# Pooling K and V in two chunked parts, six column copies per unit, and one pair's copies made a unit later or earlier, in a pooled attention with a top-1 mixture of experts

## The chip, the core and the metric

The kernel runs on one core of one Trainium2 chip. The time is the device time of one launch in microseconds (us). The core has a matrix engine (PE), a vector engine (DVE), a scalar engine (ACT), GpSimd (POOL) and a queue engine (SP) that here only issues DMAs. Each engine works through its own list of instructions strictly in order, and waits on semaphores for the others. A wait at the head of such a list holds everything behind it.

## The reference

```python
def _attn_ref(q, k, v):                       # (8, 8, 576, 64) each
    B, H, S, D = q.shape
    Sp = S // 8
    scale = 1.0 / np.sqrt(D)
    k_p = k.reshape(B, H, Sp, 8, D).mean(axis=3)
    v_p = v.reshape(B, H, Sp, 8, D).mean(axis=3)
    scores = scale * np.matmul(q, k_p.transpose(0, 1, 3, 2))
    scores = scores - np.max(scores, axis=-1, keepdims=True)
    attn = np.exp(scores)
    attn = attn / (np.sum(attn, axis=-1, keepdims=True) + 1e-09)
    return np.matmul(attn, v_p)
def _moe_ref(x, w_gate, w1, w2):              # x (4608, 512), 8 experts, F = 1024
    logits = x @ w_gate
    expert_idx = np.argmax(logits, axis=1)
    ...                                       # softmax, gate_w of the chosen expert
        h = np.maximum(x_sorted[lo:hi] @ w1[e], 0.0)
        y_sorted[lo:hi] = h @ w2[e]
    ...
    return (gate_w[:, None] * y)
```

Attention runs over keys and values that are means of eight rows. Its output, one row per token, goes through the one expert that a gate picks.

## The kernel before

**Two stages.** The attention stage takes roughly the first 200 us. It is a loop over 36 units: four pairs of batches, nine units a pair. Units 9g to 9g+3 hold the first batch of pair g, the next four the second batch, and the ninth the left-over rows of both. The loop's steps are numbered the same way below ("unit 18" is the first unit of batch 4). Six units (later four and two) make a routing group: their tokens' experts are found and their rows scattered to a buffer in HBM by expert. After that come blocks of 256 rows of one expert each, the expert stage, in a loop on the chip.

**The order of work** is written out by hand. A table of hooks says at which unit and at which place in it a step is issued: `"q"` at the unit's start (pooling on POOL), `"pe"`, `"act"`, `"dve"` in it, `"sp"` after the product with V. Small steps of routing and of V's columns stand in a list of fillers, and `fill()` issues the next one at set places. At every first unit of a routing group (6, 12, 18, 24, 30), `u_nrm` calls `drain`, which issues all that is left of an earlier group's fillers at once, and what stands ahead of them too.

**K and V of a batch.** `load_kv` (L250, L253) brings 1.1 MB of K or V into one of three buffers. `pool` (L328) adds eight rows to one on POOL, in three adds that halve the data: 1280, 640 and 320 numbers per partition. It is called in two parts, in two successive units. Batches 2 to 7 are pooled this way, K and V apart, so twelve times. Then PE turns the result (`k_pe`, `v_pe`), and `u_pe`, `u_dve` fold the gate's weights into V: `v_dve` (L402), `cross` (L418), `gather`, `high`, `low` (L429). `low` runs on POOL, and is the last step that makes `vc`. This text calls it `low` of a batch.

**V's columns.** The product with V needs `vc` spread out by head into one of three buffers `VB`. That is twelve small DMAs a batch, in the list `moves`, which `low` fills. A thirteenth one copies half of K's block (`bd<-bd`). After a unit's loads, the loop issues up to four of these (eight from unit 30 on) on SP. All loads of K, V, q (`load_q`, L257) and weights (`wload`, L102) are issued by SP too, in program order. Before unit 30 nothing but this order decides what a load stands behind.

**Also on POOL:** scatters of rows (`scatter`, L701 and L702), parts of the splits of weights into two half-precision parts (`wsplit`, L124 and L125), and `apart` (L605, L606): a pair of memsets put between two scatters when no pooling and no split came between them.

**Early block.** Under a condition that holds here, SP reads the first block of rows (L917) in unit 29, between the copies of batch 7.

Of the kernel before, what the change touches and what calls it, by code (L numbers as in the profile page):

```python
# [13 lines left out]
OP = mybir.AluOpType  # L14
# [18 lines left out]
def kernel(  # L33
# [10 lines left out]
    nc = tc.nc  # L44
    B, H, S, D = q.shape
# [182 lines left out]
    def row(x):  # L228

        return x[..., 0:ID].rearrange("p j (h x) -> p j h x", x=HW)[..., 0:D]  # L230

    def col(h):
        return h.rearrange("p j (h x) -> p j h x", x=D)
# [38 lines left out]
    for c in range(5):  # L272
        src = w_gate.rearrange("(h d) e -> d h e", d=D)[:, HS[c]:HS[c] + 3, :]
# [26 lines left out]
    moves = []  # L300

    def fill(n=1):
        while n and fillers and not fillers[0][1]:
            fillers.pop(0)[2]()
            n -= 1

    def fill_pe():
        if fillers and fillers[0][1]:
            fillers.pop(0)[2]()
# [9 lines left out]
    t1 = st[:, 0:1280].rearrange("p (c x) -> p c x", c=5)  # L319
    t2 = st[:, 1280:1920].rearrange("p (c x) -> p c x", c=5)  # L320
# [6 lines left out]

    def pool(src, dst, what=(0, 1)):  # L328
        last_pool[:] = []
        if 0 in what:  # L330
            nc.gpsimd.tensor_tensor(t1, src[:, :, 0:4 * D], src[:, :, 4 * D:], op=OP.add)
        if 1 in what:
            nc.gpsimd.tensor_tensor(t2, t1[:, :, 0:2 * D], t1[:, :, 2 * D:], op=OP.add)
            nc.gpsimd.tensor_tensor(dst, t2[:, :, 0:D], t2[:, :, D:], op=OP.add)

    def pool_now(src, dst, part):
# [128 lines left out]
    def g_qt(G, j):  # L465
        b, r = units[groups[G][0]]
        pq = psA.tile([128, 512], F32, name="pq", bufs=2)
        for x in range(4):
            if r is None:
                src = ql[(b // 2) % 2][:, 2 * x:2 * x + 2, :].rearrange("p h d -> p (h d)")  # L470
            else:
                src = qt[b % 2][:, 4 * j + x, r:r + 2, :].rearrange("p r d -> p (r d)")
            nc.tensor.transpose(pq[:, x * 128:(x + 1) * 128], src, ident)
        if j == 0:
            QT[G] = work.tile([128, 8, 128], F32, name="qT", bufs=2)
        nc.scalar.activation(QT[G][:, 4 * j:4 * j + 4, :].rearrange("p h t -> p (h t)"), pq, AF.Copy)
# [4 lines left out]
    def g_s(G, j):  # L481
        b, r = units[groups[G][0]]
        ps = psA.tile([128, 512], F32, name="ps", bufs=2)
        t = QT[G]
        if r is None:
            for x in range(2 * j, 2 * j + 2):
                for s in range(2):
                    bd = BD[(b + s) % 3].rearrange("p s h x -> p (s h) x")
                    rhs = bd[:, 2 * x:2 * x + H + 2:H + 1, :]
                    nc.tensor.matmul(ps[64 * s:64 * s + 64, (x % 2) * 2 * KP:(x % 2 + 1) * 2 * KP],  # L490
                                     t[:, x, 64 * s:64 * s + 64], rhs, start=True, stop=True)
            slots = [(4 * j + x, 0) for x in range(4)]
        else:
            hs = range(2 * j, 2 * j + 2)
            for x, h in enumerate(hs):
                nc.tensor.matmul(ps[:, x * 2 * KP:(x + 1) * 2 * KP], t[:, h, :],  # L496
                                 BD[b % 3][:, :, h, :], start=True, stop=True)
            slots = [(h, s) for h in hs for s in range(2)]
        PS_[G, j] = (ps, slots)
        if j == stages(G) - 1:  # L500
            QT.pop(G)

    def g_min(G, j):
        ps, slots = PS_[G, j]
        nmx = work.tile([128, 4], F32, name="nmx", bufs=4)
        nc.vector.tensor_reduce(nmx, ps[:, 0:4 * KP].rearrange("p (h x) -> p h x", x=KP), axis=AX.X, op=OP.min)  # L506
        PS_[G, j] = (ps, nmx, slots)

    def g_exp(G, j):
        ps, nmx, slots = PS_.pop((G, j))  # L510
        for x, (h, s) in enumerate(slots):
            p = pbuf[groups[G][s] % 4]
            nc.scalar.activation(p[:, h * KP:(h + 1) * KP], ps[:, x * KP:(x + 1) * KP], AF.Exp,  # L513
                                 bias=nmx[:, x:x + 1], scale=-1.0)

    def u_pt(i):
        p = pbuf[i % 4]
        pp = psA.tile([128, 1024], F32, name="pp")
        for c in range(5):
            nc.tensor.transpose(pp[:, c * 128:(c + 1) * 128], p[:, c * 128:(c + 1) * 128], ident)  # L520
        ph = work.tile([128, 640], F16, name="ph")
        nc.scalar.activation(ph, pp[:, 0:640], AF.Copy, scale=SP)
        PP_[i] = (pp, ph)

    def u_lo(i):
        pp, ph = PP_[i]
        pl = work.tile([128, 640], F16, name="pl", bufs=1)
        nc.vector.scalar_tensor_tensor(pl, pp[:, 0:640], SP, ph, op0=OP.mult, op1=OP.subtract)
        PP_[i] = (ph, pl)
# [67 lines left out]
    def flush(n=99, upto=99):  # L597
        while n and pend and pend[0][0] <= upto:
            _, f, u = pend.pop(0)
            f(u)  # L600
            n -= 1
# [143 lines left out]
    def pooled(n, b):  # L745
        KVS[n, b] = work.tile([128, 5, D], F32, name=n, bufs=2)
        return kv[(2 * b + (n == "vp")) % 3], KVS[n, b]
# [11 lines left out]
    src, vp = pooled("vp", 0)  # L759
# [55 lines left out]
    def put(i, pos, f, *a):  # L815
        assert 0 <= i < NU
        hooks.setdefault((i, pos), []).append((f, a))

    def prep(b, k, v, u):
        put(k[0], "pe" + k[1], k_pe, b)  # L820
        put(k[0], "act" + k[1], k_act, b)
        put(v[0], "pe" + v[1], v_pe, b)
        put(v[0], "act" + v[1], v_act, b)
        put(u[0], "pe" + u[1], u_pe, b)
        put(u[0], "dve", u_dve, b)
# [9 lines left out]
    for g in range(NPAIR):  # L835
        u0 = 9 * g
        e, o = 2 * g, 2 * g + 1
        if g:
            for b, at, last in ((e, u0 - 11, u0 - 8), (o, u0 - 7, u0 - 3)):
                first = 1 if (g == 1 and b == e) else 0  # L840
                for f, x in ((pool_k, 0), (pool_v, 2)):
                    if first:
                        put(1 + x // 2, "q", f, b, 0)
                        put(1 + x // 2, "q", f, b, 1)
                    else:
                        put(at + x, "q", f, b, 0)
                        put(at + x + 1, "q", f, b, 1)
                    n = 2 * b + x // 2 + 3
                    if n < 2 * B:
                        put(at + x + 4, "sp", load_kv, *order[n])  # L850
                if first:
                    prep(b, (3, "2"), (4, ""), (5, ""))
                else:
                    prep(b, (last, ""), (last + 1, ""), (last + 2 + (b == o), ""))
        if g + 1 < NPAIR:
            put(u0 + 1, "sp", load_q, e + 2)
            put(u0 + 6, "sp", load_q, o + 2)
            put(u0 + 5, "sp", load_ql, g + 1)
# [79 lines left out]
    def run(i, pos):  # L938
        for f, a in hooks.pop((i, pos), []):
            f(*a)  # L940

    def routes(i):
        gidx, u = GOF[i]
        if u == bounds[gidx][1] - 1:
            return route(gidx)
# [33 lines left out]
    for i in range(NU):  # L979
        A, Z = halves.get(2 * i), halves.get(2 * i + 1)  # L980
        Y = halves.get(2 * i - 1)
        run(i, "q")
        flush(1)
        if i:
            u_pt(i)
        if A:
            g_s(*A)
        if Y:
            g_exp(*Y)
        if i in turns:  # L990
            g_qt(*turns[i])
        if (i, "pe") not in hooks:
            fill_pe()
        run(i, "pe")
        if i:
            u_lo(i)
        if A:
            g_min(*A)
            fill()
            g_exp(*A)  # L1000
        fill()
        run(i, "act")
        run(i, "dve")
        if i:
            u_pv(i)
        run(i, "pe2")
        if i == 29:
            KVS["late"] = 1
        if len(pend) > 2:
            flush(1)  # L1010
        fill_pe()
        run(i, "sp")
        for _ in range(min(4 if i < 30 else 8, len(moves))):
            nc.sync.dma_start(*moves.pop(0))
        if Z:
            g_s(*Z)
        u_nrm(i, (lambda: g_min(*Z)) if Z else None)
        run(i, "act2")
        run(i, "dve2")
        last = routes(i)  # L1020
        fill(2 if i >= NU - 3 else 1)
# [177 lines left out]
    for j in range(2):  # L1199
        x, h, l = row(xg[:, j:j + 1]), col(xh[:, j:j + 1, 0]), col(xh[:, j:j + 1, 1])  # L1200
# [114 lines left out]
```

## Time and profile before

| | us |
|---|---|
| median of 3 runs | 645.25 |
| lowest, highest | 642.09, 645.43 |
| the profiled execution's own time | 646.38 |
| its span, first to last instruction | 644.4 |

The span is what the trace covers. The 2 us between it and the execution's own time lie around the program. The profiled execution is 1.1 us above the median of the runs. Times "at" some us below count from the start of the span.

### The profile page before, as it was taken

To read this page: it belongs to the slowest core of one execution; us is meant where nothing else is said; L and a number is where in the kernel's file an instruction comes from. 1 tells how busy PE (TensorE), PEld (TensorE's weight loads), DVE (VectorE), ACT (ScalarE), POOL (GpSimd) and SP (SyncE) were. 2 spreads that over 40 slices of the span, in tenths; PEclk is the share of its full clock that TensorE was granted. 3 is DMA by queue.
4 is the path that set the end of the run, shared out by engine and by line. 5 is a ranking of instruction groups with operands and counts; after the bars stand their busy time and mean duration, and the time that the engine had idled before them with its cause. 6 is when DMAs were issued, how large, how long until landed. Compare 5 with 4: busy or idle time off the path is not lost. (4 is left out here: it accounts for less than half of the span.)

```text
span 644.4 us, 15871 instructions
## 1 busy us (share of the span) xinstructions
PE 579.3 (90%) x4694; PEld 422.3 (66%) x4695; DVE 316.9 (49%) x619; ACT 286.8 (45%) x635; POOL 276.4 (43%) x532
## 2 busy tenths in 40 slices
PE   6888898787977698998899999999999989999994
PEld 5777788676865275675566667766667666677662
DVE  7577678886675417221773755122722262221212
ACT  2576688677651226222672753122722352221222
POOL 6799689998684323112314123222121232012212
PEclk9798999899899699999899999999999989999998
DMA  8997789858476565963689497533231333213200
GB/s 244 290 287 222 231 231 311 266 176 248 168 214 232 192 120 152 384 164 85 168 247 327 108 321 251 153 102 77 42 81 53 96 72 102 49 57 79 65 16 30
DMA packets 104203, 108.15 MB, mean 168 GB/s; under 512 B 62310, under 2 KB 72550, under 8 KB 104168
## 3 DMA queue, kind: packets, MB, share of 16 engines
q1 hardware_dynamic: 97528, 86.72, 47.9%
q0 software_dynamic: 6640, 20.99, 8.8%
q8 instruction: 19, 0.31, 0.2%
q14 instruction: 16, 0.13, 0.1%
HBM read 72.99 MB, written 23.37 MB: 150 GB/s over the span
## 5 line engine op out<-in xcount | busy, mean ns | idle before, releaser
L1039 PEld LDWEIGHTS <-bd 128*128 128x128 f16 x936 | 91.6, 99 | 110.1 <-issue 3.6
L1224 POOL TENSOR_TENSOR spacer<-ql,iG 1x1 f32<-1x1 f32 x44 | 23.8, 540 | 218.9 <-ACT ql L1220 218.0
L1033 DVE SCALAR_TENSOR_TENSOR bd<-ps,bd 128x512 f16<-128x512 f32 x44 | 30.2, 690 | 151.3 <-ACT bd L1029 149.5
L1033 DVE SCALAR_TENSOR_TENSOR bd<-pp,bd 128x512 f16<-128x512 f32 x44 | 30.3, 691 | 100.7 <-ACT bd L1029 100.7
L513 ACT ACTIVATE both<-ps,nmx 128x72 f32<-128x72 f32 x288 | 69.0, 330 | 23.9 <-DVE nmx L506 23.3
L1029 ACT ACTIVATE bd<-pp 128x512 f16<-128x512 f32 x44 | 26.2, 597 | 116.8 <-PE pp L969 74.3
L1039 PE MATMUL po<-w,bd 128*128 128x512 f16 x264 | 59.1, 379 | 0.8 <-ACT bd L1029 0.8
L1029 ACT ACTIVATE bd<-ps 128x512 f16<-128x512 f32 x44 | 26.1, 597 | 74.8 <-PE L967 46.1
L1039 PE MATMUL po<-kv,bd 128*128 128x512 f16 x264 | 58.9, 379 | 0.3 <-ACT bd L1029 0.3
L1225 POOL DMA_INDIRECT out_dram<-ql,iG x44 | 43.8, 995 | 21.5 <-issue 20.2
L496 PE MATMUL ps<-bd,qT 128*128 128x144 f32 x256 | 47.0, 310 | 3.5 <-DMA bd<-bd 1.9
L967 PE MATMUL ps<-kv,qt 128*128 128x256 f16 (+1 forms) x176 | 45.7, 267 | 4.9 <-issue 3.2
L1039 PE MATMUL pq<-kv,bd 128*128 128x512 f16 x216 | 48.1, 379 | 0.0
L969 PE MATMUL ps<-kv,qt 128*128 128x256 f16 (+1 forms) x176 | 45.6, 267 | 1.9 <-DVE qt L118 1.9
L967 PE MATMUL ps<-kv,w 128*128 128x256 f16 (+1 forms) x176 | 43.8, 262 | 3.1 <-DVE kv L118 2.8
L969 PE MATMUL ps<-kv,w 128*128 128x256 f16 (+1 forms) x176 | 43.8, 262 | 2.5 <-DVE w L118 2.5
L968 PE MATMUL ps<-kv,qt 128*128 128x256 f16 (+1 forms) x176 | 45.7, 267 | 0.0
L1039 PE MATMUL pq<-w,bd 128*128 128x512 f16 x192 | 45.3, 395 | 0.3 <-remote 0.3
L554 PE MATMUL po<-vb,ph 128*128 128x146 f16 (+2 forms) x384 | 33.4, 234 | 12.6 <-DMA vb<-vc 7.0
L969 PE MATMUL pp<-kv,qt 128*128 128x256 f16 (+1 forms) x176 | 44.7, 263 | 0.0
L968 PE MATMUL pp<-kv,qt 128*128 128x256 f16 (+1 forms) x176 | 44.7, 263 | 0.0
L967 PE MATMUL pp<-kv,qt 128*128 128x256 f16 (+1 forms) x176 | 44.7, 263 | 0.0
(236 smaller groups left out, 1335.8 us busy)
## 6 DMA issues: line engine op xcount, KB each, us to landing
both<-in_moe_w_dram SPq DMA_DIRECT2D x6, 2048.0 KB, 11.7
st<-in_moe_w_dram SPq DMA_DIRECT2D x6, 2048.0 KB
vb<-x_by_expert SPq DMA_DIRECT2D x17, 578.0 KB
st<-in_moe_w_dram SPq DMA_DIRECT2D x8, 1024.0 KB
kv<-in_k_dram SPq DMA_DIRECT2D x7, 1024.0 KB
kv<-in_v_dram SPq DMA_DIRECT2D x7, 1024.0 KB
qt<-in_q_dram SPq DMA_DIRECT2D x6, 1024.0 KB
qt<-in_q_dram SPq DMA_DIRECT2D x4, 512.0 KB
```

Source lines behind the costliest of these rows:

```text
L496: nc.tensor.matmul(ps[:, x * 2 * KP:(x + 1) * 2 * KP], t[:, h, :], BD[b % 3][:, :, h, :], start=True, stop=True)
L513: nc.scalar.activation(p[:, h * KP:(h + 1) * KP], ps[:, x * KP:(x + 1) * KP], AF.Exp, bias=nmx[:, x:x + 1], scale=-1.0)
L554: nc.tensor.matmul(po[:, half, cols], a[:, c * 128:(c + 1) * 128], VB[b % 3][:, y, c, sl, 0:CW], start=st, stop=False, skip_group_check=True)
L967: nc.tensor.matmul(dst, wh, xT[:, d, 0:n], start=(d == 0), stop=False)
L968: nc.tensor.matmul(dst, wh, xT[:, DC + d, 0:n], start=False, stop=False)
L969: nc.tensor.matmul(dst, wl, xT[:, d, 0:n], start=False, stop=(d == DC - 1))
L1029: nc.scalar.activation(hT[0][:, 2 * k:2 * k + 2, :].rearrange("p f t -> p (f t)"), pH[k], AF.Relu)
L1033: V.scalar_tensor_tensor(l, pH[k], 0.0, h, op0=OP.max, op1=OP.subtract)
L1039: nc.tensor.matmul(y, hT[x][:, f, 128 * j:128 * j + 128], W2[s][z][:, f, :], start=(half == x == z == f == 0), stop=(half == z == 1 and f ...
L1224: nc.gpsimd.tensor_tensor(spacer[:, 0:1], ys[j][0:1, 0:1], iG[0:1, j:j + 1].bitcast(F32), op=OP.add)
L1225: st = nc.gpsimd.indirect_dma_start(out=out, out_offset=bass.IndirectOffsetOnAxis(ap=iG[:, j:j + 1], axis=0), in_=ys[j], in_offset=None, b ...
```

## The change

`pool` works by chunks: part 0 takes chunks 0 to 2 through the first two adds, and part 1 takes chunks 3 and 4 through them and then makes the last add over all five. Up to six entries of `moves` are issued per unit ahead of unit 30. In pair 2, `u_pe` and `u_dve` of batch 4 move from unit 12 to unit 13, and those of batch 5 from unit 18 to unit 17.

```diff
     def pool(src, dst, what=(0, 1)):
         last_pool[:] = []
-        if 0 in what:
-            nc.gpsimd.tensor_tensor(t1, src[:, :, 0:4 * D], src[:, :, 4 * D:], op=OP.add)
+        for x in what:
+            c = (slice(0, 3), slice(3, 5))[x]
+            nc.gpsimd.tensor_tensor(t1[:, c], src[:, c, 0:4 * D], src[:, c, 4 * D:], op=OP.add)
+            nc.gpsimd.tensor_tensor(t2[:, c], t1[:, c, 0:2 * D], t1[:, c, 2 * D:], op=OP.add)
         if 1 in what:
-            nc.gpsimd.tensor_tensor(t2, t1[:, :, 0:2 * D], t1[:, :, 2 * D:], op=OP.add)
             nc.gpsimd.tensor_tensor(dst, t2[:, :, 0:D], t2[:, :, D:], op=OP.add)
...
-                    prep(b, (last, ""), (last + 1, ""), (last + 2 + (b == o), ""))
+                    prep(b, (last, ""), (last + 1, ""), (last + 2 + ((b == o) != (g == 2)), ""))
...
-        for _ in range(min(4 if i < 30 else 8, len(moves))):
+        for _ in range(min(6 if i < 30 else 8, len(moves))):
             nc.sync.dma_start(*moves.pop(0))
```

On POOL, in units 12 to 14: `kp` ends the pooling of K of batch 5 and `vp` that of its V, `vc<-u,vc` is `low` of batch 4, and L124 and L125 are a split of weights. Before:

```order
L334 TENSOR_TENSOR kp<-st_65 128x320
L701 MEMSET spacer 1x1
L702 DMA x_by_expert<-both,rpos 38016x578
L429 TENSOR_TENSOR vc<-u,vc 128x5x8
L657 TENSOR_TENSOR both<-ids,zi 128x6
L331 TENSOR_TENSOR st_65<-kv_154 128x1280
L701 MEMSET spacer 1x1
L702 DMA x_by_expert<-both,rpos 38016x578
L713 TENSOR_TENSOR cum<-cum,rso 128x8
L333 TENSOR_TENSOR st_65<-st_65 128x640
L334 TENSOR_TENSOR vp<-st_65 128x320
L124 TENSOR_TENSOR st_65<-st_64,swc 128x1024
```

The same place in the changed kernel, from the scatter behind `kp` on (its line numbers are one higher):

```order
L703 DMA x_by_expert<-both,rpos 38016x578
L658 TENSOR_TENSOR both<-ids,zi 128x6
L332 TENSOR_TENSOR st_65<-kv_154 128x768
L333 TENSOR_TENSOR st_65<-st_65 128x384
L702 MEMSET spacer 1x1
L703 DMA x_by_expert<-both,rpos 38016x578
L332 TENSOR_TENSOR st_65<-kv_154 128x512
L333 TENSOR_TENSOR st_65<-st_65 128x256
L335 TENSOR_TENSOR vp<-st_65 128x320
L124 TENSOR_TENSOR st_65<-st_64,swc 128x1024
L125 TENSOR_TENSOR w_01_61<-st_65,w_00_60 128x1024
L430 TENSOR_TENSOR vc<-u,vc 128x5x8
```

`low` of batch 4 has moved behind the pooling of V of batch 5 and behind a whole split.

On SP, in units 18 to 20: the copies of batch 5 (`vb<-vc`), the load of q of batch 6, and the load of V of batch 7 (`kv<-in_v_dram`). Before:

```order
L257 DMA qt_155<-in_q_dram 128x8x256
L1014 DMA vb_164<-vc 72x2x72
L1014 DMA vb_164<-vc 56x2x72
L1014 DMA vb_164<-vc 16x2x72
L1014 DMA vb_164<-vc 72x2x72
L250 DMA kv_131<-in_v_dram 64x512
L253 DMA kv_131<-in_v_dram 128x4x512
L1014 DMA vb_164<-vc 40x2x72
```

In the changed kernel, from the sixth copy on:

```order
L1015 DMA vb_164<-vc 32x2x72
L257 DMA qt_155<-in_q_dram 128x8x256
L1015 DMA vb_164<-vc 72x2x72
L1015 DMA vb_164<-vc 24x2x72
L1015 DMA vb_164<-vc 48x2x72
L1015 DMA vb_164<-vc 72x2x72
L1015 DMA vb_164<-vc 8x2x72
L1015 DMA vb_164<-vc 64x2x72
L250 DMA kv_131<-in_v_dram 64x512
L253 DMA kv_131<-in_v_dram 128x4x512
```

The load of V of batch 7 stood behind four of the twelve copies, and now stands behind all twelve and behind the load of q. In the same way the load of q of batch 7 stood behind seven copies of batch 6, and now stands behind twelve.

On POOL, behind the pooling of V of batch 7 and ahead of `low` of batch 7, the rows of the changed kernel show scatters of group 2 with pairs of memsets between them:

```order
L703 DMA x_by_expert<-both,rpos 38016x578
L647 TENSOR_TENSOR rc_2407<-cum,zf 128x8
L606 MEMSET zpad 128x512
L607 MEMSET zpad 128x512
L702 MEMSET spacer 1x1
L703 DMA x_by_expert<-both,rpos 38016x578
L606 MEMSET zpad 128x512
L607 MEMSET zpad 128x512
L702 MEMSET spacer 1x1
L703 DMA x_by_expert<-both,rpos 38016x578
```

Before, these scatters stood among the pooling of batches 6 and 7, where they mostly need no pair. From the first `rpos` of group 0 to `low` of batch 7, POOL's list has 21 scatters in both kernels, 8 pairs before and 10 in the changed one.

## Rows read from the trace of the kernel before

**Rows 1.** Stretches: length; PE, PEld, DVE, ACT, POOL busy (count); clock, DMA share, GB/s.

```profile
100.00:140.00 40.00, 33.64 (x348) 30.39 (x347) 35.06 (x79) 29.38 (x99) 37.87 (x43) 0.96 0.85 267
...
223.00:644.00 421.00, 399.97 (x2930) 266.14 (x2928) 159.44 (x184) 154.50 (x206) 102.08 (x285) 0.99 0.46 131
```

**Rows 2.** PE's waits over the span: us in total, times, longest.

```profile
PE po L554 <- DMA vb<-vc: 7.0, 5, 2.9
...
PE pq L473 <- DVE ut L418: 2.6, 1, 2.6
...
PE pq L380 <- POOL vp L334: 2.0, 1, 2.0
```

**Rows 3.** PE in order of time: start, us, what [idle before, releaser].

```profile
114.83 0.76 PE L554 MATMUL po<-vb,ph 128*128 128x219 f16 x8 [0.43 <-DMA vb<-vc]
...
120.23 0.66 PE L473 MATMUL pq<-ident,qt 128*128 128x128 f32 x4 [2.65 <-DVE ut L418]
...
156.73 0.66 PE L473 MATMUL pq<-ident,qt 128*128 128x128 f32 x4 [0.72 <-DMA qt<-in_q_dram]
...
161.32 1.55 PE L554 MATMUL po<-vb,ph 128*128 128x146 f16 x9 [2.93 <-DMA vb<-vc]
...
181.44 0.58 PE L554 MATMUL po<-vb,ph 128*128 128x73 f16 x7 [0.66 <-DMA vb<-vc]
```

**Rows 4.** POOL's groups by shape, 20 to 215 us: busy us, mean ns | idle before.

```profile
L331 POOL TENSOR_TENSOR st<-kv 128x1280 f32<-128x1280 f32 x12 | 35.1, 2921 | 0.1
L333 POOL TENSOR_TENSOR st<-st 128x640 f32<-128x640 f32 x12 | 19.8, 1649 | 0.4
...
L334 POOL TENSOR_TENSOR kp<-st 128x320 f32<-128x320 f32 x6 | 5.2, 864 | 0.5
...
L605 POOL MEMSET zpad<- 128x512 f32 x9 | 4.9, 541 | 0.0
...
L324 POOL TENSOR_TENSOR st<-kv 128x256 f32<-128x256 f32 x2 | 1.5, 728 | 0.0
...
L326 POOL TENSOR_TENSOR vp<-st 128x64 f32<-128x64 f32 x1 | 0.3, 322 | 0.1
```

**Rows 5.** POOL in order of time.

```profile
70.38 0.19 POOL L692 CAST rpos<-rpf 128x6 int32<-128x6 f32 x1 [3.50 <-DVE rpf L677]
...
91.14 0.25 POOL L429 TENSOR_TENSOR vc<-u,vc 128x40 f16<-128x40 f32 x1 [1.64 <-DVE vc L426]
...
100.19 2.13 POOL L125 TENSOR_TENSOR w<-st,w 128x1024 f16<-128x1024 f32 x1
...
120.88 0.27 POOL L429 TENSOR_TENSOR vc<-u,vc 128x40 f16<-128x40 f32 x1
...
137.56 2.93 POOL L331 TENSOR_TENSOR st<-kv 128x1280 f32<-128x1280 f32 x1
...
166.33 0.26 POOL L429 TENSOR_TENSOR vc<-u,vc 128x40 f16<-128x40 f32 x1 [4.59 <-DVE vc L426]
```

**Rows 6.** SP's issues in order of time.

```profile
104.73 3.86 SPq L1014 DMA_DIRECT2D vb<-vc  x5
...
124.69 0.54 SPq L250 DMA_DIRECT2D kv<-in_v_dram  x1
...
150.18 0.47 SPq L257 DMA_DIRECT2D qt<-in_q_dram  x1
...
166.62 3.44 SPq L1014 DMA_DIRECT2D vb<-vc  x4
171.70 0.37 SPq L917 DMA_DIRECT2D vb<-x_by_expert  x1
172.31 7.80 SPq L1014 DMA_DIRECT2D vb<-vc  x8
```

**Rows 7.** DVE's `v_dve` of batches 5 and 7 in order of time.

```profile
116.34 3.64 DVE L402 SCALAR_TENSOR_TENSOR vc<-vp,vc 128x320 f16<-128x320 f32 x1
...
164.04 0.49 DVE L402 SCALAR_TENSOR_TENSOR vc<-vp,vc 128x320 f16<-128x320 f32 x1 [0.23 <-DMA st<-in_moe_w_dram]
```

## The prediction

> **What bounds the kernel now.** I read the stretches first. The expert stage from 223 us on has PE busy for 400.0 of 421 us [rows 1], and the change does not touch it: what the attention stage gains or loses arrives at the end one to one, as long as nothing later absorbs it. In the attention stage (100 to 140 us) PE is busy 33.6 of 40 us, but POOL 37.9 [rows 1]. The reader should see two engines close to full, and PE not the fuller one.
>
> Then PE's waits, for what a unit stalls on. The product with V waits 7.0 us in five places for copies into `VB`, and 2.6 us once for `cross` behind `v_dve` [rows 2]. In time they lie at 114.83 (batch 4), 120.23 (`cross`), 161.32 (batch 6, with 0.72 for a load of q just ahead) and 181.44 (batch 7) [rows 3]. These are what the change could win.
>
> Then POOL in order of time, because `low` on POOL releases the copies. It waits 3.50 us at 70.38, 1.64 us at `low` of batch 4 and 4.59 us at `low` of batch 7 [rows 5]. Between 70.4 and 161.7 us (166.33 less 4.59) the 1.64 us is by far its longest wait, so there POOL's time is the sum of its own list. Last, SP's issues: a copy costs SP 0.8 to 1.0 us (3.86 us for five, 3.44 for four, 7.80 for eight [rows 6]). Twelve take about 10.3 us at 0.86, as long as two units (nine lie between the gates of batches 4 and 6, 46.5 us [rows 3]). So SP is a narrow place that "six per unit" does not widen; it only changes what stands ahead of what.
>
> So the chain that I follow is: POOL's list, `low`, SP's issues, landing, product with V. The last such gate, batch 7, sets where the attention stage ends.
>
> **Part 1, pooling by chunks.** The same numbers are added, in five adds for three. From 64 to 256 numbers an add grows from 0.322 to 0.728 us [rows 4]: 2.1 ns a number and 0.19 us fixed. The two more adds cost 0.37 us and two gaps of some 0.04 us: 0.45 us a pooling (estimate), 5.4 us over twelve. Bounds: 0.3 (gaps overlap) to 0.7 (each new add meets a blocked port, as the 640-number add does on average: 1.649 us against 1.54 by the slope). The first two poolings end just ahead of `v_pe` of batch 2, for which PE already waits 2.0 us [rows 2]: +0.9. The next ones vanish in the wait of 3.50 us at 70.38 [rows 5], except that this wait is for DVE, which has become 0.9 later. From there seven more poolings lie ahead of `low` of batch 7: +3.2.
>
> **Part 2, the order on POOL.** Two more pairs of memsets ahead of `low` of batch 7, 1.07 us each (0.541 for the first [rows 4], its twin alike): +2.1. `low` of batch 4 no longer waits 1.64 us for DVE: -1.6. Before, POOL was ready for `low` of batch 7 at 161.7; now at 161.7 + 0.9 + 3.2 + 2.1 - 1.6 = 166.3, plus any wait for a load.
>
> **Part 3, SP's order.** The load of V of batch 7 went out at 124.69 [rows 6]. It now stands behind all twelve copies of batch 5 and a load of q. `low` of batch 5 was at 120.88 [rows 5]; I put it at 121.5 (0.9 and four poolings later, the 1.6 and a scatter earlier, perhaps 1 us for a late load). Then 10.3 us of copies, 0.5 for q, 1.1 for two issues: out at 133.4. Its 1.1 MB at 267 GB/s [rows 1] need 4.3 us: landed at about 138. POOL wants it at 136.6 (15.1 us of its list after 121.5: two second parts at 3.0, a first part 2.9, a split 4.1, a scatter and small steps 2.1; before, it began that add at 137.56 [rows 5]). Wait: 1.5 us, bounds 0 and 4. So `low` of batch 7 comes at 166.3 + 1.5 = 167.8 instead of 166.33. DVE's share of it is in time: see part 5.
>
> From the first copy of batch 7 (166.62) to the end of the last (172.31 + 7.80 = 180.11) SP took 13.5 us with the early block between [rows 6], and PE went on 1.3 us later, at 181.44 [rows 3]. The new order is 6, block, 6 instead of 4, block, 8: the same 13.5 us. PE goes on at 167.8 + 0.3 + 13.5 + 1.3 = 182.9: **+1.5 us**.
>
> **Part 4, batch 4.** `low` moves from 91.14 to behind the split that ends at 102.3 [rows 5]. With the shifts above it runs at about 102.7. Six copies (5.2), q and V of batch 6 (1.7), six copies (5.2): the last is issued at 114.8, and stands behind 2.1 MB that go out from 108 on and need 8 us at 267 GB/s [rows 1]. I take landing at 117, bounds 116 and 119; PE went on at 114.83 [rows 3]. A new stall of about 2 us, then. Behind it the wait of 2.65 us for `cross` of batch 5 [rows 3] goes, because `u_dve` now comes ahead of the drain in unit 18. Net about -0.6 by unit 20. I count it as nothing at the end: batches 5 to 7 are gated by POOL and SP as above.
>
> **Part 5, batch 6.** Its twelve copies go out in a row, so the 2.93 us at 161.32 goes. But the load of q of batch 7, issued at 150.18 before [rows 6], waits behind them: `low` at about 141.7, 10.3 of copies, 1.5 for left-over rows, out at 153.5. It landed 6.5 us after its issue before (156.73 [rows 3]); with 4.5 to 6.5 now, PE waits for q until 158 to 160, and starts the product 1.7 us later (161.32 less 2.93, less 156.73), at 160 to 162 against 161.32. The stall changes its name and keeps its size. DVE needs 5 us from there to `low` (161.32 to 166.33): 165 to 167, ahead of POOL's 167.8.
>
> **Sum.** 646.38 + 1.5 = 647.9 for the profiled execution, which lies 1.1 above the median of the runs; on the median, 645.25 + 1.5 = 646.8. A measurement of this kernel can tell about 0.5%, 3.2 us, from no change.
>
> **Rivals.**
>
> *No move at the end (645.2).* POOL waited 4.59 us at `low` of batch 7 [rows 5]. If the load of V is in time and the poolings cost 0.3, the added 4 us just fill that wait. For it: the two numbers are equal within my error. Against it: the load of V has nearly no slack.
>
> *Shorter adds free DVE (642.6).* `v_dve` of batch 5 took 3.64 us at 116.34, that of batch 7 took 0.49 with POOL idle [rows 7]; a 1280-number add of 2.92 us [rows 4] ran through the first. POOL's longest pooling add falls to 1.8 us, so a blocked DVE instruction ends at least 1.1 us sooner, and batch 5's is moved away too. If these waits set the pace rather than the copies, PE keeps the 2.65 us [rows 3]: 645.25 - 2.65. Against it: the next gate, batch 5's copies, is not earlier. The Trainium skill, "SBUF — State Buffer", section "Who interferes with whom", says that a DVE instruction with two SBUF inputs and a GpSimd instruction that reads SBUF exclude each other: whichever starts first holds the shared port for its whole length. By that rule the chunks are a gain; the 3.64 us agrees with it.
>
> *Copies on time (636 to 641).* If all waits for copies (7.0 us) and the 2.6 us [rows 2] go and nothing takes their place, 9.6 us: 635.7; half of it, 640.5. For it: batch 6 and 7 stalls follow copies issued late. Against it: SP's 0.86 us a copy does not change, and POOL's list gets longer.
>
> *Loads starve POOL (650.8).* The mechanism of part 3 at its far end: V of batch 6 lands 1.5 us after POOL wants it (it stands in the same queue behind batch 4's late copies), V of batch 7 4 us after. `low` of batch 7 is 5.5 us later. It decides as soon as the load of V of batch 7 lands after 137; each microsecond past that is one at the end.
>
> **How the numbers follow.** Forecast 0.38, nearly all of it within 0.5% (0.06 beyond it); no move 0.16; shorter adds 0.10 (about a fifth of it past -0.5%, with batch 6's stall gone in part); copies on time 0.16, all past it; starved POOL 0.20, most of it past +0.5%. With some weight for a late step that I have not seen, this gives faster 0.20, same 0.50, slower 0.30. The range from 640 (half of the copies' waits gone) to 651 (POOL starved) leaves out less than 2 in 10; the likeliest case's own range is 644 to 649.
>
> **What would show it.** Right: five adds a pooling, 5.6 to 5.8 us in all; `low` of batch 4 after 102 us; PE waiting 3 us or more for copies at batch 4, none for `cross` in unit 19; a wait for q in place of that for copies at unit 27; POOL waiting at the first add of V of batch 7; `low` of batch 7 at 167 to 169 without a wait for DVE. Wrong: `low` of batch 7 well before 166, or PE past batch 7's gate before 179: then POOL's list was not the bound.

## The result, and the profile after

The changed kernel takes 649.11 us (median of 20 runs, 644.99 to 655.86). The kernel before, run beside it, takes 644.21 us (20 runs, 636.4 to 648.3). The ratio is 1.0108, with a 95% interval of 1.008 to 1.0135: **slower by 1.1%**. The forecast was 646.8 us and "no measurable change". The ratios leave out the few executions that fell in a slower state, so they can differ a little from the quotient of two medians. The profiled execution below took 654.56 us, 5.4 above its median; a second profile of the same kernel (`a_again` below) took 651.31 and shows the same three waits for V, each within 1 us, so the reading does not hang on that one execution.

The stretches first, with the columns of [rows 1].

```profile
100.00:140.00 40.00, 30.81 (x309) 27.74 (x309) 30.63 (x73) 26.36 (x89) 33.27 (x41) 0.91 0.68 210
223.00:652.00 429.00, 403.55 (x2926) 268.77 (x2923) 160.16 (x185) 155.21 (x208) 102.97 (x287) 0.97 0.45 132
```

POOL, the fullest engine before, is now busy 33.27 of 40 us instead of 37.87, PE 30.81 instead of 33.64, and the transfers fell from 267 to 210 GB/s. No engine took over: all of them wait more. POOL's waits say for what (total, times, longest), and PE's beside them answer to [rows 2].

```profile
POOL st L332 <- DMA kv<-in_v_dram: 11.6, 3, 4.8
```

```profile
PE po L555 <- DMA vb<-vc: 7.7, 5, 4.2
PE pq L474 <- DMA qt<-in_q_dram: 6.0, 3, 3.3
...
PE ps L497 <- DMA bd<-bd: 4.9, 2, 4.7
```

POOL's first line is new; [rows 4] has 0.1 us at the same add. The 2.6 us for `cross` on PE are gone, as forecast, and 6.0 us for loads of q stand in their place (1.2 before). POOL in order of time, which answers to [rows 5] (L430 is `low`, L332 the first add of a pooling):

```profile
79.42 0.27 POOL L430 TENSOR_TENSOR vc<-u,vc 128x40 f16<-128x40 f32 x1
...
93.70 1.82 POOL L332 TENSOR_TENSOR st<-kv 128x768 f32<-128x768 f32 x1 [3.07 <-DMA kv<-in_v_dram]
...
104.96 0.44 POOL L430 TENSOR_TENSOR vc<-u,vc 128x40 f16<-128x40 f32 x1
...
123.51 1.80 POOL L332 TENSOR_TENSOR st<-kv 128x768 f32<-128x768 f32 x1 [4.80 <-DMA kv<-in_v_dram]
...
127.58 0.27 POOL L430 TENSOR_TENSOR vc<-u,vc 128x40 f16<-128x40 f32 x1
...
146.68 1.81 POOL L332 TENSOR_TENSOR st<-kv 128x768 f32<-128x768 f32 x1 [3.74 <-DMA kv<-in_v_dram]
...
149.59 0.25 POOL L430 TENSOR_TENSOR vc<-u,vc 128x40 f16<-128x40 f32 x1
...
176.48 0.27 POOL L430 TENSOR_TENSOR vc<-u,vc 128x40 f16<-128x40 f32 x1
```

The lines of `low` are batches 3 to 7, and the waits are for V of batches 5, 6 and 7. The last `low` went from 166.33 [rows 5] to 176.48, and no longer waits for DVE. Why V is late stands in SP's issues, which answer to [rows 6].

```profile
87.60 0.39 SPq L253 DMA_DIRECT2D kv<-in_v_dram  x1
...
97.02 0.62 SPq L102 DMA_DIRECT2D st<-in_moe_w_dram  x1
105.43 6.08 SPq L1015 DMA_DIRECT2D vb<-vc  x6
111.61 0.53 SPq L257 DMA_DIRECT2D qt<-in_q_dram  x1
112.19 0.60 SPq L250 DMA_DIRECT2D kv<-in_v_dram  x1
112.83 0.58 SPq L253 DMA_DIRECT2D kv<-in_v_dram  x1
113.45 6.14 SPq L1015 DMA_DIRECT2D vb<-vc  x6
...
127.88 5.01 SPq L1015 DMA_DIRECT2D vb<-vc  x6
132.93 0.58 SPq L257 DMA_DIRECT2D qt<-in_q_dram  x1
133.62 4.82 SPq L1015 DMA_DIRECT2D vb<-vc  x6
138.49 0.60 SPq L250 DMA_DIRECT2D kv<-in_v_dram  x1
...
149.87 4.90 SPq L1015 DMA_DIRECT2D vb<-vc  x6
...
156.73 4.84 SPq L1015 DMA_DIRECT2D vb<-vc  x6
161.67 0.54 SPq L257 DMA_DIRECT2D qt<-in_q_dram  x1
...
176.78 5.04 SPq L1015 DMA_DIRECT2D vb<-vc  x6
183.41 0.39 SPq L918 DMA_DIRECT2D vb<-x_by_expert  x1
184.11 4.99 SPq L1015 DMA_DIRECT2D vb<-vc  x6
```

From 97.64 to 105.43 SP issues nothing. It stands at the first copy of batch 4, which needs `low` (104.96), and q and V of batch 6, which need nothing from it, stand behind. V goes out at 112.19, not at 102.22 as in SP's issues before:

```profile
98.25 3.35 SPq L1014 DMA_DIRECT2D vb<-vc  x4
...
102.22 0.59 SPq L250 DMA_DIRECT2D kv<-in_v_dram  x1
```

Of these 10.0 us, 7.2 are the later start of the copies that stand ahead of the loads in their unit (105.43 for 98.25), and 2.8 come from their being six instead of four. POOL wants V from 118.71 (123.51 less 4.80). V of batch 5 is late without that hole: its large piece goes out at 87.60 (83.90 before), behind six copies of batch 3 for four, and SP waits 1.7 us between its two pieces. The DMA view of 95 to 145 us shows the hole: GB/s in 40 slices of 1.25 us.

```profile
GB/s 114 120 405 302 233 360 415 279 20 30 12 4 239 31 272 241 327 318 289 316 412 345 157 39 162 382 399 202 43 17 251 77 229 380 203 49 121 300 405 261
```

The ninth to twelfth slices, 105 to 110 us, carry 4 to 30 GB/s: the loads issued up to 97.64 are through, and SP is busy with the six small copies of batch 4. Then the held loads come together: V of batch 6 lands 10.7 us after its large piece was issued (112.83 to 123.51). PE at the places of [rows 3], with the wait for q of batch 6 in the place of that for `cross`:

```profile
119.02 0.63 PE L474 MATMUL pq<-ident,qt 128*128 128x128 f32 x4 [2.21 <-DMA qt<-in_q_dram]
...
124.06 1.57 PE L555 MATMUL po<-vb,ph 128*128 128x146 f16 x9 [4.21 <-DMA vb<-vc]
...
168.93 0.66 PE L474 MATMUL pq<-ident,qt 128*128 128x128 f32 x4 [3.26 <-DMA qt<-in_q_dram]
...
190.43 0.95 PE L555 MATMUL po<-vb,ph 128*128 128x73 f16 x7 [0.68 <-DMA vb<-vc]
```

Batch 4's product resumes at 124.06 (114.83 before) and the load of q of batch 7 is used at 168.93 (156.73 before). Batch 7's gate opens at 190.43 instead of 181.44, 9.0 us later, and the span grows by 7.5 us (644.4 to 651.9).

### The profile page after: what moved, and what is told of

Same layout as the page of the kernel before. It is cut to its first block, busy times and chain, and to the rows that moved or that the text cites. A ratio compares the mean times of both kernels' runs of the same rounds, so it can differ in the third digit from the quotient of the medians.

```text
span 651.9 us, 15885 instructions
## 1 busy us (share of the span) xinstructions
PE 585.4 (90%) x4694; PEld 428.6 (66%) x4695; DVE 317.6 (49%) x619; ACT 286.7 (44%) x635; POOL 283.2 (43%) x560
## 5 line engine op out<-in xcount | busy, mean ns | idle before, releaser
L497 PE MATMUL ps<-bd,qT 128*128 128x144 f32 x256 | 48.5, 317 | 6.4 <-DMA bd<-bd 4.9
L968 PE MATMUL ps<-kv,w 128*128 128x256 f16 (+1 forms) x176 | 45.6, 273 | 8.3 <-DMA kv<-bd 5.5
L968 PE MATMUL ps<-kv,qt 128*128 128x256 f16 (+1 forms) x176 | 46.9, 272 | 5.1 <-issue 3.6
L970 PE MATMUL ps<-kv,qt 128*128 128x256 f16 (+1 forms) x176 | 46.7, 271 | 1.6 <-DVE qt L118 1.6
L970 PE MATMUL ps<-kv,w 128*128 128x256 f16 (+1 forms) x176 | 45.6, 273 | 2.6 <-DVE w L118 2.6
L969 PE MATMUL ps<-kv,qt 128*128 128x256 f16 (+1 forms) x176 | 46.9, 272 | 0.0
L969 PE MATMUL ps<-kv,w 128*128 128x256 f16 (+1 forms) x176 | 45.7, 273 | 0.0
```

The costliest lines, as they stand in the source:

```text
L968: nc.tensor.matmul(dst, wh, xT[:, d, 0:n], start=(d == 0), stop=False)
L969: nc.tensor.matmul(dst, wh, xT[:, DC + d, 0:n], start=False, stop=False)
L970: nc.tensor.matmul(dst, wl, xT[:, d, 0:n], start=False, stop=(d == DC - 1))
```

## The experiments

Two theories stood at the start. **Theory A**: SP holds loads behind copies that are gated by `low`; V (and q) land late, POOL waits, the next `low` is late, and with it the next copies and loads. **Theory B**: POOL's list is longer by itself (more adds, more memsets). Each kernel ran beside the kernel before, on the same chip. A ratio is to that kernel, with its 95% interval; under 1 is faster. Where the times of `low` of two profiles are compared, count from `low` of batch 3 as well: it already lies anywhere between 78.05 and 84.43 us, before most of what is studied here. From it to `low` of batch 7 it is 87.3 us in the kernel before and 97.1 in the changed one.

### One part alone

The four kernels are the kernel before with one hunk of the change: the chunks (`c1_chunks`), six copies (`c2_six`), both moves (`c3_move`), or, from the hunk of the moves, batch 5's move alone:

```diff
-                    prep(b, (last, ""), (last + 1, ""), (last + 2 + (b == o), ""))
+                    prep(b, (last, ""), (last + 1, ""), (last + 2 + (b == o and g != 2), ""))
```

> The kernel before with the chunked pooling alone. Theory A (loads of K, V and q go out late because SP's list puts more in front of them, so POOL waits for V): the order on SP is unchanged, so no wait of POOL for V appears; the 0.45 us a pooling mostly fill POOL's 4.59 us of waiting at low of batch 7: -1 to +2 us against before. Theory B (the longer list on POOL is the loss): 5 us, nearly the whole loss of the changed kernel.

> The kernel before with six copies a unit alone. Theory A: the loads of V of batches 5 and 7 and of q of batches 6 and 7 stand behind more copies; POOL waits 2 to 4 us for V of batch 5 and of batch 7, none of 4.8 us for V of batch 6; +2 to +5 us. Theory B: POOL's list is as before, copies go out earlier: 0 to -5 us.

> The kernel before with the copies' making of batches 4 and 5 moved alone. Theory A: low of batch 4 runs at about 102 us instead of 91; SP stands still at its copies, and q and V of batch 6 go out 4 to 6 us later than at 101.7 and 102.2; POOL waits 1 to 4 us for V of batch 6; +1 to +4 us. Theory B: two pairs of memsets, and 1.64 us of waiting less: +0.5 us.

> The kernel before with the making of batch 5's copies moved from unit 18 to 17, and batch 4's left where it was. Theory A: the wait of 2.65 us for cross at unit 19 goes and nothing on SP is later: 0 to -3 us. Theory B: 0 (POOL's list has the same work).

Measured (kernel before: 651.23 us on this chip): chunks 1.0048 [1.0015, 1.008], six copies 1.0109 [1.0068, 1.015], both moves 1.0055 [1.0021, 1.009], batch 5's move 1.0011 [0.9975, 1.0048]. No part is a gain, and the sum of three, 2.1%, is about twice what they cost together. The chunks cost 2.8 us by the medians with no wait for V, between what A (up to 2) and B (5) had expected. Six copies alone cost as much as the whole change, more than A's 2 to 5 us, though POOL hardly waits for V there (0.2 us, expected 2 to 4 in two places). Instead PE waits for q of batch 7 (PE in order of time, `c2_six`):

```profile
161.92 1.11 PE L473 MATMUL pq<-ident,qt 128*128 128x128 f32 x4 [5.15 <-DMA qt<-in_q_dram]
```

So theory A, told of V alone, is too narrow. This profile cannot show where the median's loss lies, though: the execution took 651.97 us, 6.6 below the median of its kernel (658.61).

### One part taken out, and the loads given their place back

`d1_no_move`, `d3_no_chunks` and `d2_no_six` are the changed kernel without one part, and `a_again` is the changed kernel once more. `e1_early_loads` is the whole change and one line:

```diff
-                        put(at + x + 4, "sp", load_kv, *order[n])
+                        put(at + x + 3, "sp", load_kv, *order[n])
```

> The changed kernel again, so that its parts stand beside it on one chip: 0.8 to 1.4% over before by both theories.

> The changed kernel without the move of batches 4 and 5. Theory A (loads of K, V and q go out late on SP): q of batch 7 still stands behind twelve copies, PE waits 3 to 5 us for it; low of batch 4 is back at about 94 us, so POOL's wait of 4.8 us for V of batch 6 goes; +0.9 to +1.4%, like six copies alone. Theory B (POOL's longer list): what the chunks alone cost, +0.5%.

> The changed kernel with the pooling of before. Theory A: SP's order is that of the changed kernel, so POOL waits three times for V, 8 to 14 us together, and low of batch 7 comes after 173 us; +0.8 to +1.2%, little better than the changed kernel. Theory B: POOL's list is 5 us shorter; +0.3% or less.

> The changed kernel with every load of K and V hooked one unit earlier, ahead of copies that it stood behind. Theory A: POOL's waits for V fall from 11.6 us to 4 or less, low of batch 7 comes 4 to 8 us earlier than in the changed kernel; q of batch 7 still stands behind the copies and PE still waits for it; 3 to 6 us faster than the changed kernel. Theory B: as slow as the changed kernel.

> The changed kernel with four copies per unit as before: pooling by chunks and both moves stay. Theory A6, that six copies per unit are what puts the loads late: nearly all of the loss goes, ratio 0.998 to 1.005 to the kernel before, POOL's waits for V under 3 us in all. Theory A, that any of the parts makes the loads late by moving low and the copies behind it: 1.006 to 1.012, as with the other two parts taken out, and POOL's waits for V stay.

Measured: again 1.0117 [1.007, 1.0165]; without the moves 1.0106 [1.0053, 1.0159]; without chunks 1.0106 [1.0069, 1.0143]; without six copies 1.0025 [0.999, 1.0061]; with early loads **1.002 [0.999, 1.0049]**, 643.77 us against 650.7 for the same change on the same chip. POOL's list is as long in the last, so theory B as the whole loss falls; up to 0.5%, the end of the interval, may still be the list's. `d3_no_chunks` says the same from the other side: its adds are those of before, theory B expected 0.3% or less, and the loss stays. POOL waits 2.71, 4.23 and 4.17 us there at the first adds of V of batches 5, 6 and 7 (the profile puts the second down to the DMA `bd<-bd`). Nor is it the clock of PE: from 100 to 140 us the granted clock was 0.91 in the changed kernel (0.96 before), and 0.91 in `e1_early_loads` too.

In `e1_early_loads`, V of batch 6 goes out at 97.69, ahead of `low` of batch 4 (first rows SP), and POOL's waits for V shrink to one (second rows, POOL in order of time):

```profile
97.69 0.62 SPq L250 DMA_DIRECT2D kv<-in_v_dram  x1
...
154.14 0.55 SPq L257 DMA_DIRECT2D qt<-in_q_dram  x1
```

```profile
101.62 0.26 POOL L430 TENSOR_TENSOR vc<-u,vc 128x40 f16<-128x40 f32 x1
...
121.60 0.27 POOL L430 TENSOR_TENSOR vc<-u,vc 128x40 f16<-128x40 f32 x1
...
137.87 1.81 POOL L332 TENSOR_TENSOR st<-kv 128x768 f32<-128x768 f32 x1 [0.58 <-DMA kv<-in_v_dram]
...
141.97 0.26 POOL L430 TENSOR_TENSOR vc<-u,vc 128x40 f16<-128x40 f32 x1 [0.94 <-DVE vc L427]
...
168.85 0.27 POOL L430 TENSOR_TENSOR vc<-u,vc 128x40 f16<-128x40 f32 x1
```

The last `low` comes at 168.85, against 176.37 in `a_again`: 7.5 us, about as much as the medians differ (6.9). From `low` of batch 3 it is 89.8 us. The edit moves every load of K and V, so it does not part the two; but the waits that it takes away on POOL are those for V. The kernel without six copies shows the same cure from the other side: POOL waits 1.57 us for V, once, and `low` of batch 7 is at 171.23, 90.8 us after that of batch 3.

`d1_no_move` shows a second road. There POOL never waits for V, and yet `low` of batch 7 comes at 175.31 (first rows POOL, then SP, then PE, each in order of time):

```profile
147.84 0.27 POOL L430 TENSOR_TENSOR vc<-u,vc 128x40 f16<-128x40 f32 x1
...
175.31 0.25 POOL L430 TENSOR_TENSOR vc<-u,vc 128x40 f16<-128x40 f32 x1 [7.67 <-DVE vc L427]
```

```profile
160.17 0.54 SPq L257 DMA_DIRECT2D qt<-in_q_dram  x1
```

```profile
167.97 1.11 PE L474 MATMUL pq<-ident,qt 128*128 128x128 f32 x4 [6.97 <-DMA qt<-in_q_dram]
```

POOL stands ready and waits for DVE, DVE for PE, PE for q of batch 7. That load went out at 160.17, 12.3 us after `low` of batch 6 (147.84), behind twelve copies. With four per unit it stands behind seven in the kernel before (141.69 to 150.18) and eight in `d2_no_six` (144.12 to 152.63), 8.5 us after `low` in both. So six copies per unit put four or five more copies ahead of this load.

These copies are about half of the delay, and alone they need not cost anything. Counted from `low` of batch 3, the load goes out 8.2 us later in `d1_no_move` than before: 3.8 for the copies, and 4.4 because `low` of batch 6 is itself later, without any wait for V; why was not followed. In `e1_early_loads` the load stands behind twelve copies as well (154.14, 12.2 us after `low` of batch 6), but that `low` is at 141.97, and PE hardly waits, against what was expected:

```profile
161.38 0.66 PE L474 MATMUL pq<-ident,qt 128*128 128x128 f32 x4 [0.33 <-DMA qt<-in_q_dram]
```

### Is an earlier load a gain anyway, and is a later one a loss?

`g1_before_early` and `g2_before_late` are the kernel before with that one number at 3 and at 5. "Theory C" in the expectation: earlier loads pay in any case.

> The kernel before, unchanged but that every load of K and V in the attention stage is hung one unit earlier in SP's order (x + 3 for x + 4). In the kernel before, POOL never waits for such a load, so theory A (the change is slow because loads stand behind copies and come late to POOL) says that earlier loads have nothing to give here: ratio 0.997 to 1.003 to the kernel before, low of batch 7 within 2 us of where it is without the edit. Theory C, that earlier loads are simply a gain of 5 to 7 us for any kernel of this shape, and that the change's own cost is untouched by them, says 0.989 to 0.992.

> The kernel before, unchanged but that every load of K and V is hung one unit later in SP's order (x + 5 for x + 4): neither pooling, nor copies per unit, nor the making of V's columns is touched. Theory A says that this alone makes POOL wait for V by several us at batches 5 to 7, moves low of batch 7 from 166 us to 172 or later and costs 0.8 to 2%: ratio 1.008 to 1.02. Theory B (POOL's longer list) and any theory in which DVE or the copies themselves cost the time say 0.998 to 1.003.

Measured: early 1.0027 [1.0, 1.0055], late 1.0126 [1.0092, 1.016]. Earlier loads give the kernel before nothing, so theory C falls: what `e1_early_loads` wins is what the change had lost. (`low` of batch 7, expected within 2 us of 166.33, was at 171.30 in that profile; but that of batch 3 was already 3.4 us late, and between them lie 88.9 us against 87.3.) One unit later costs as much as the whole change, with no part of it made. But the road is not the one that theory A gave. POOL's waits for late loads are 0.22 and 0.40 us; PE waits for the copy of half of K's block, which SP issued at 75.06 just after a 1 MB load of K (PE in order of time, `g2_before_late`):

```profile
88.06 1.30 PE L496 MATMUL ps<-bd,qT 128*128 128x144 f32 x4 [11.57 <-DMA bd<-bd]
```

The ratio is as theory A said, and its account of POOL missed. What the run shows is that the loads' place among the copies is worth 1.3% by itself.

### Combinations

`e3_early_move5` is the change with early loads and batch 5's move alone, repeated as `e3_again`. `e4_early_q` is the change with early loads, q of odd batches two units earlier (`u0 + 4` for `u0 + 6`). `f2_move5_early_q` is `e3` with q of batches 4 and 6 one unit earlier (`u0 + (g == 0)` for `u0 + 1`). `f1_six_early` is the kernel before with six copies and early loads; `f3_six_early_q` adds both earlier loads of q. `f4_early_no_six` is `e3` with four copies.

> The changed kernel with loads of K and V one unit earlier, and with batch 4's making of V's columns back at its old unit (only batch 5's is moved). Theory A: the remaining stall of batch 4's late copies goes as well, and nothing waits for V: 0.992 to 1.000 against the kernel before. If batch 4's place does not matter once the loads are early, it comes out as the changed kernel with early loads did: 1.000 to 1.004.

> The changed kernel with loads of K and V one unit earlier, and with the load of q of each odd batch two units earlier (u0 + 4 for u0 + 6), so that q of batch 7 goes out ahead of batch 6's last copies. With early K and V alone PE waited only 0.3 us for that load, so if low of batch 7 hangs on POOL alone, this changes nothing: 1.000 to 1.004 against the kernel before. If the late q is a second brake in the same queue, it gains 1 to 3 us: 0.996 to 1.000. If the earlier load of q pushes V back on SP, it loses: 1.004 or more.

> The kernel before with six copies per unit and with the loads of K and V one unit earlier. Six copies alone cost 1.1% with hardly a wait of POOL for V. If that cost, too, is loads (V, K or q) that come late behind copies, the earlier hook takes most of it away: 0.998 to 1.005. If it is the copies themselves (their traffic, or what they do to the load of q, whose place is not changed here), it stays: 1.006 to 1.013.

> The changed kernel with loads of K and V one unit earlier, batch 4's making of V's columns at its old unit, and the load of q of each even batch from the third pair's on one unit earlier (u0 for u0 + 1). In the kernel without this last edit PE waited 6.7 us at 121.9 us for q of batch 6, which had gone out at 113.1. If that wait counts at the end: 0.986 to 0.994 to the kernel before. If it only moves to the next gate (low of batch 7, at 168.6 us there, hangs on POOL), no further gain: 0.993 to 0.999.

> The kernel before with six copies per unit, K and V loaded one unit earlier, and q as well (even batches from the third pair's on one unit, odd batches two units earlier). If what six copies still cost beside early K and V (0.8%) is a load of q that stands behind them, that goes: 0.996 to 1.003. If it is the copies' own, it stays: 1.006 to 1.011.

> The changed kernel with K and V loaded one unit earlier, batch 4's making of V's columns at its old unit, and four copies per unit. If six copies per unit are a cost wherever they stand, this beats the same kernel with six, by 0.3 to 0.8%: 0.988 to 0.993. If they pay once the loads are ahead of them, it is slower than with six: 0.998 to 1.004.

> The changed kernel with K and V loaded one unit earlier and batch 4's making of V's columns at its old unit, once more. If its lead is its own: 0.993 to 0.9985. If it was the chance of one chip: 0.9985 to 1.003.

| kernel | us, before beside it | ratio [95%] |
|---|---|---|
| `e3_early_move5` | 640.59, 643.57 | 0.9958 [0.9931, 0.9985] |
| `e3_again` | 641.17, 642.06 | 0.9976 [0.9939, 1.0013] |
| `f2_move5_early_q` | 640.8, 643.4 | 0.9983 [0.9951, 1.0014] |
| `f4_early_no_six` | 644.91, 642.06 | 1.0005 [0.9963, 1.0046] |
| `e4_early_q` | 643.83, 643.57 | 1.002 [0.9994, 1.0047] |
| `f3_six_early_q` | 645.25, 642.06 | 1.0029 [0.9984, 1.0074] |
| `f1_six_early` | 646.6, 643.4 | 1.0079 [1.0043, 1.0115] |

`e3` (and `f2`, which is `e3` with earlier q) is the one version ahead of both kernels: 0.2 to 0.4%, the first interval clear of 1, the repeat's not. Its `low` of batch 7 is at 168.62 (166.82 in the repeat), and POOL's waits for K or V there are 2.12 us for K in one profile and 0.91 for V in the other. Earlier q adds nothing to it or to `e1` (`f2`, `e4`): there the last `low` hangs on POOL, without a wait. Without six copies its lead is gone by the middle value, but the intervals overlap. `f1` still costs 0.8%, against theory A with K and V alone; with q earlier too the middle value falls to 0.3%, and PE's waits for q from 9.1 to 0.7 us. That fits the second road, but the intervals overlap and the medians lie equally far above their partners (3.2 us each), so this stays open.

One number of the profiles sorts nearly all of these kernels: when PE passes the gate of batch 7. In the changed kernel, `a_again`, `d1`, `d3` and `g2`, which lose 1.06 to 1.26%, it is at 188.4 to 193.2 us; in the others, which lose 0.8% or less or gain, it is at 178.8 to 186.3 (181.44 before). Only `c2_six` does not fit, with 183.51 at 1.1%; its profiled execution is the one 6.6 us below its median.

## Why the prediction was wrong, point by point

**The step that failed** is the term "plus any wait for a load" of parts 2 and 3, mis-sized: "perhaps 1 us for a late load" ahead of `low` of batch 5, and 1.5 us for V of batch 7. Ahead of `low` of batch 5 it measured 3.07 and 4.80 us, at V of batches 5 and 6, and at V of batch 7 3.74: together 11.6 us. The rival "Loads starve POOL" had the mechanism, at a chance of 0.20 and 650.8 us, and named V of batch 6 behind batch 4's copies; the waits came out at twice the 5.5 us that it took for its far end. The range held the median; the forecast of no measurable change did not.

The other terms held within 1 us. The first poolings cost less than the 0.9 us forecast: `low` of batch 3, with one more pooling behind it, is 0.39 later. Two rows of POOL before, in order of time (the first is `low` of batch 3, the second the first add of V of batch 6):

```profile
79.03 0.27 POOL L429 TENSOR_TENSOR vc<-u,vc 128x40 f16<-128x40 f32 x1
...
116.73 2.89 POOL L331 TENSOR_TENSOR st<-kv 128x1280 f32<-128x1280 f32 x1
```

Summed from `low` of batch 3 (79.03 before, 79.42 after) to that of batch 7, a sum of measured rows: 0.39 of lead, six poolings at 0.41, 2.14 for two pairs of memsets, 11.6 of waits, less the 1.64 and 4.59 us of waits for DVE that are gone [rows 5]: 10.4 us. Measured: 166.33 to 176.48, 10.15. (One reading was too strong: beside the 1.64 us, which was to be "by far" the longest wait, POOL has one of 0.96 us at 156.12. No term hangs on it.)

**Part 1** held. The groups by shape, 20 to 215 us (busy us, mean ns | idle before):

```profile
L332 POOL TENSOR_TENSOR st<-kv 128x768 f32<-128x768 f32 x12 | 22.0, 1833 | 11.6 <-DMA kv<-in_v_dram 11.6
L332 POOL TENSOR_TENSOR st<-kv 128x512 f32<-128x512 f32 x12 | 15.5, 1290 | 0.1
L333 POOL TENSOR_TENSOR st<-st 128x384 f32<-128x384 f32 x12 | 12.2, 1013 | 0.9
L333 POOL TENSOR_TENSOR st<-st 128x256 f32<-128x256 f32 x12 | 10.1, 844 | 0.9
```

Together 4.98 us a pooling, against 2.921 + 1.649 before [rows 4]: 0.41 more, forecast 0.45. With the last add it is 5.8 us for K and 6.0 for V (5.6 to 5.8 had been named).

**Part 3** is where it broke. V of batch 7 was to go out at 133.4 and went out at 138.49; the 1.5 us of wait became 3.74, with POOL wanting it at 142.94, not 136.6. Both slips are one: `low` of batch 5 was at 127.58, not 121.5, for the waits at V of batches 5 and 6. Then a second error. I took a load's time from its bytes over the mean rate (4.3 us a megabyte, 8 for two); issued close to other loads, V of batch 6 took 10.7 us, and V of batch 7 7.5 (139.18 to 146.68). From `low` of batch 7 to its gate it took 13.95 us, against the 15.1 forecast.

**Part 4** had the order right and the times 2 to 7 us early: `low` at 104.96 (forecast 102.7), V of batch 6 out at 112.19 (108), PE on at 124.06 (117, bounds 116 and 119). I costed it as a stall of PE that heals by unit 20. It does not stay on PE: the copies that wait for `low` hold the loads behind them, and POOL gets the bill.

**Part 5** had the mechanism: a wait for q in place of that for copies. It measured 3.26 us at 168.93 instead of 158 to 160, since `low` of batch 6 was itself 7.9 us later than the 141.7 taken. The Trainium skill, "DMA: Bandwidth & Descriptors", section "Queues, rings and completion order", says that each DMA engine takes a queue's descriptors in ring order but may complete them otherwise. By that rule, on each engine, whatever stands behind twelve copies also starts after them. No run here shows the order inside an engine; the traces show the step before it: SP issues this load 12.1 us after `low` behind twelve copies, and 8.5 behind seven or eight.

**The rivals.** "No move at the end" fell with the load of V. "Shorter adds free DVE": the 3.64 us of `v_dve` of batch 5 [rows 7] did go (0.49 us at 115.47 after), but the same instruction of batch 5 also took 0.49 in `c2_six`, where the adds are as long as before; and chunks alone are a loss of 0.5%. Nor does the trace bear out "the 3.64 us agrees with it" in full: `v_dve` started at 116.34, ahead of the add at 116.73, and it was the add that ran its usual 2.89 us. "Copies on time" got the reverse: the waits for copies grew to 7.7 us.

**Not settled**: why the parts are not additive; why chunks alone cost 0.5%; what part of the six copies' cost is q; and how the two roads, V to POOL and q to PE, share the loss. At `low` of batch 7 DVE was done at 175.46 (166.25 before) and POOL at 176.48 (161.74 before), within 1 us of each other. The two are not independent: q of batch 7 stands behind `low` of batch 6, and that comes behind the waits for V. Nor is it followed why `f2`, whose batch 7's gate opens 4.1 us ahead of that of `e3` (178.75, 182.88), has the same span of 638.4 us.

## What to carry to other kernels

A queue that works in order has one price per issue and another per wait at its head. Before more issues are let through per step, or a gate is moved later, list every load that stands behind the gated item, when its user wants it, and how early it goes out; here leads of 14.5 and 12.9 us (V of batches 6 and 7, from the issue of the first piece to when POOL wants it) became 6.5 and 4.5, and the loads took 11.3 and 8.2, counted from the same issue. Where such a change loses, move the loads ahead of the gate first: one number gave back nearly all that three parts had cost (1.0117 to 1.002), and gave the kernel before nothing.

## What the runs showed of the hardware

Loads of the same size took very different times, and a small copy took longer than any of those below. 1 MB of q took 6.5 us from issue to use in the kernel before (150.18 to 156.73); 1 MB of V took 10.7 us in the changed kernel where 1 MB of q had been issued 1.2 us ahead, and 7.5 us where 1 MB of weights was issued 1.2 us behind it, while 4.3 us had been worked out from the mean rate. A copy of 144 KB issued 1.2 us behind a load of 1 MB was first used 13.0 us after its issue (75.06 to 88.06, `g2_before_late`). In each case the user stood waiting for it. And the DMA engines were nearly idle for 5 us (4 to 30 GB/s) while loads stood ready behind copies on SP: there the transfers were not the limit, the order of issue was.
